# Windowed attention and a gated feed-forward layer: the down projection of tile pairs by Strassen's scheme, behind the ups, with a transposed output

## The chip, the core and the metric

One core of a Trainium2 chip. The metric is the device time in microseconds (us) of one execution, as the median of several runs. The core's engines are called as in the profile: PE (TensorE, matrix products; PEld is its weight load), DVE (VectorE), ACT (ScalarE, activations and copies), POOL (GpSimd), SP (SyncE, which starts the transfers here). The working memory is SBUF; PE writes to PSUM, eight banks of 128 x 512 float32.

## The reference

Eight batches and eight heads, 576 positions, head size 64, float32. Attention looks back over a window of 64 positions; its output, 4608 tokens of 512 numbers, is the input of a gated layer with 1536 hidden features.

```python
scores = scale * np.matmul(q, k.transpose(0, 1, 3, 2))
...
mask = (rel >= 0) & (rel < window)
scores = np.where(mask, scores, -1000000000.0)
scores = scores - np.max(scores, axis=-1, keepdims=True)
attn = np.exp(scores)
attn = attn / (np.sum(attn, axis=-1, keepdims=True) + 1e-09)
return np.matmul(attn, v).astype(np.float32)
...
x = np.ascontiguousarray(attn_out.transpose(0, 2, 1, 3)).reshape(B * S, H * D)
...
gate = 1.0 / (1.0 + np.exp(-(x @ w_gate)))
val = x @ w_val
return (gate * val @ w_out).astype(np.float32)
```

## The kernel before

**Tiles.** The tokens are cut into 12 tiles of 384 (`TT`), and these into 6 pairs. Activations stand feature by token: 128 features on the partitions, 384 tokens along the row. The 1536 hidden features are 12 blocks of 128, `j`; block `k` and block `k + 6` go together in a pair's products, so there are `NK` = 6 rounds. Every float32 operand of a large product is split in a high part (what PE's float32r format holds) and a low part, the rest. A product is three matmuls: high by high, high by low, low by high. A split is one copy (ACT) and one subtraction (DVE or POOL).

**Attention.** One unit is two heads of one tile, four units a tile. `stage_s` issues the scores on PE, and with them the outputs of the unit before; DVE takes the maxima (L232), ACT six exponentials (L241); `stage_n` divides by the sums (L259, POOL or DVE); `stage_b` transposes on PE (L290) and copies on ACT (L295); the outputs become the tile's input `xf`. The units of pair s + 1 are put between the products of pair s at planned places (`fill`, `attend`).

**The plain pair.** Pair 0 (tiles 0 and 1) is computed directly: `up` (L340) takes 12 matmuls of 128x384 for one block of gate or value, `gate_table` (L369) the sigmoid from ACT's table, `hidden_split` (L380) the two parts of the hidden block, `down` (L410) adds block j to the output of one group of 128 tokens: the hidden block is stationary, 512 columns of `w_out` move, three matmuls of 128x512. Tile 1's hidden blocks go to DRAM (`hd`) and come back when tile 0 has left its output banks. Beside this the weights, which arrive as float64, are converted (`conv_load` to `conv_c`, L97 to L143), and gate and value are written to DRAM as float32 (`w32d`) and in parts (`wd`).

**The five other pairs** take both up projections by Strassen's scheme in Winograd's form (`PRODUCTS`, L443): gate and value weights of round k are a 2 x 2 matrix of blocks (features by hidden features), the inputs of the two tiles another (features by tokens), and seven products of sums of blocks take the place of eight. A product is two halves of three matmuls of 128x384 (L579). The sums of the weights are made once, in the plain pair and in pair 1, on POOL (`sums_load`, `sums_make`, `sums_split`, `sums_store`, L477 to L528), in pieces of 128x128, and written to `wd`; later pairs read `wd` (`w_load`, seven buffers `W`). The input sums are made by `x_parts`, `x_part` and `x_rest`. In each round the seven products of the gate (m = 0) come first, then the seven of the value (m = 1), on three PSUM banks (`psum(s, b)`). `product` adds the results together on DVE (L585) and `result` makes of them a gate or a hidden block. In pairs 2 to 4 the gate is not the sigmoid: `gate_act` (L358) makes it of Relu, Tanh and Exp on ACT, a mask and a multiply on DVE, twice too large, which the output's copy makes good (L433).

**Their down projections** are plain ones. Tile a's (a = 2s) stand one after the other between the next round's products, on the other three banks; tile b's follow the last round (`last_tile`, L720), its hidden blocks split just ahead by `hidden_b` (L626). All 12 blocks of `w_out` stay in SBUF (`wo`).

**What sets the order.** The program is a list of events with planned times and a rank (`put`), sorted. PE keeps the order of the list (`keep_in_program_order`); the other engines' queues come from a scheduler which works on the list, with chains that hold ACT's table functions in order (`table_order`) and `issue_after`. SP starts all transfers in the order of its own queue, so a transfer that waits holds back those behind it.

## Time and profile before

| what | us |
|---|---|
| median of 3 runs (lowest to highest) | 1000.32 (999.86 to 1002.28) |
| span of the profiled execution | 997.6 |
| PE busy in it | 979.2 |
| start: attention of tiles 0 and 1, first weights | 0 to 48 |
| plain pair | 48 to 215 |
| pairs 1 to 5 begin at | 215, 377, 536.5, 696.5, 856.5 |
| down matmuls L419, all (804 + 402 + those of other forms) | 251.2 + 158.8 in the two large groups |
| transfers | 208.92 MB |

The profile shows one execution. The page's head gives the busy time of each engine; its groups name a line, an engine, an operation and the tiles (out<-in), with the number of instructions, the busy time and the mean time of one, and behind the bar the idle time of the engine just ahead of them with what ended it. The chain of work lists, from its start, what the end of the span depended on. A wait row reads "who L.. <- whom: us, count, longest". A table of windows has a row for each stretch and in it the busy time of every engine, the granted clock of PE (1.00 is full), the share in which the 16 DMA engines were busy, and what they moved. A matmul that is pipelined behind another costs PE the distance between their starts, which is less than the mean time that the groups give.

### The profile page before, as it was taken

Reading aid. Unit: us, or ns where it says so; the run is one execution under the profiler, and the core shown is the slowest. Engines: PE = TensorE matmul, PEld = TensorE weight load, DVE = VectorE, ACT = ScalarE, POOL = GpSimd, SP = SyncE. Lnnn points to the kernel's source line nnn. Section 1 sums busy time; section 2 is a strip of 40 time slices with the busy share of each in tenths; the row PEclk is TensorE's granted clock in tenths of the full one; section 3 lists DMA queues with packets and bytes.
Section 4 is the critical chain, followed back from the end, with each engine's and each line's share of the span. In section 5 each row is a group of like instructions: output and inputs, shape, how many; then the busy total and the mean of one; then the engine's idle time right before and its main releaser. Section 6 shows DMA issues by size and latency. Waiting matters only on the chain.

```text
span 997.6 us, 19847 instructions
## 1 busy us (share of the span) xinstructions
PE 979.2 (98%) x6984; PEld 884.1 (89%) x6984; DVE 633.0 (63%) x1737; ACT 530.5 (53%) x1433; POOL 253.5 (25%) x360
## 2 busy tenths in 40 slices
PE   7999999999999999999999999999999999999998
PEld 5888999889899889999988999988999997999996
DVE  7899888536665656666674666565666667344532
ACT  7888878544755646555545455464564464211122
POOL 4200124337674031112241122113212124010100
PEclk9999999999999999999999999999999999999999
DMA  9999888478786606766734776651776651466500
GB/s 336 320 346 364 321 286 278 144 258 292 262 259 219 221 33 225 228 218 218 219 108 130 229 233 209 213 196 38 242 237 214 203 187 56 161 224 195 190 32 32
DMA packets 84338, 208.92 MB, mean 209 GB/s; under 512 B 9360, under 2 KB 24976, under 8 KB 84240
## 3 DMA queue, kind: packets, MB, share of 16 engines
q1 hardware_dynamic: 84240, 207.66, 63.1%
q8 instruction: 56, 0.92, 0.4%
q14 instruction: 42, 0.34, 0.1%
HBM read 165.94 MB, written 41.68 MB: 208 GB/s over the span
## 4 chain that ended last, share of the span: by engine, by line
PE 84%; ACT 6%; DVE 4%; DMA 2%; issue 1%; DVEq 0%; ACTq 0%; SPq 0%
PE pr L579 40%; PE y L419 29%; PE ph L349 7%; PE s L208 3%; ACT p L241 3%; PE pp L290 3%; DMA w32d<-w 1%; PE s L319 1%; PE oo L319 1%; ACT g L362 1%; ACT e L361 1%; DVE p L232 1%; DMA wd<-w 1%; PE pr L319 1%; DVE u L585 0%
## 5 line engine op out<-in xcount | busy, mean ns | idle before, releaser
L419 PE MATMUL y<-w,hh 128*128 128x512 f32 x804 | 251.2, 393 | 0.0
L579 PE MATMUL pr<-x_T,wt 128*128 128x384 f32 x1152 | 226.4, 338 | 0.5
L579 PEld LDWEIGHTS pr<-x_T,wt 128*128 128x128 f32 x1152 | 202.2, 188 | 11.1 <-DVE u L585 4.3
L579 PE MATMUL pr<-x_B,wt 128*128 128x384 f32 x864 | 176.4, 340 | 0.2
L419 PEld LDWEIGHTS y<-w,hh 128*128 128x128 f32 x804 | 148.8, 189 | 21.8 <-ACT hh L384 1.4
L419 PE MATMUL y<-w,hl 128*128 128x512 f32 x402 | 158.8, 395 | 0.0
L579 PEld LDWEIGHTS pr<-x_B,wt 128*128 128x128 f32 x864 | 150.6, 188 | 8.2 <-issue 2.6
L585 DVE TENSOR_TENSOR u<-pr,p 128x384 f32<-128x384 f32 x120 | 66.5, 554 | 139.4 <-PE pr L579 138.8
L259 POOL TENSOR_TENSOR p<-p,rs 128x384 f32<-128x384 f32 x76 | 65.4, 875 | 288.2 <-DVE rs L250 197.4
L241 ACT ACTIVATE p<-p,mn 128x128 f32<-128x128 f32 x288 | 111.1, 393 | 27.1 <-DVE mn L232 26.3
L388 POOL TENSOR_TENSOR hl<-h,hh 128x384 fp32r<-128x384 f32 x48 | 50.0, 1042 | 283.8 <-DVE hh L386 283.8
L349 PE MATMUL ph<-x,w 128*128 128x384 f32 x576 | 105.9, 338 | 0.0
L349 PEld LDWEIGHTS ph<-x,w 128*128 128x128 f32 x576 | 99.7, 188 | 2.0 <-issue 1.0
L419 PEld LDWEIGHTS y<-w,hl 128*128 128x128 f32 x402 | 75.6, 188 | 18.3 <-DVE hl L388 2.1
L232 DVE CUSTOM_DVE_ANT_0 p<-s,m 128x128 f32<-128x128 f32 x288 | 66.3, 286 | 21.9 <-PE s L208 21.9
L585 DVE TENSOR_TENSOR c<-pr,u 128x384 f32<-128x384 f32 x120 | 66.7, 556 | 10.9 <-ACT g L372 4.8
L388 DVE TENSOR_TENSOR hl<-hb,hh 128x384 fp32r<-128x384 f32 x60 | 39.7, 673 | 41.2 <-ACT hh L384 40.7
L295 ACT COPY pT<-pp 128x384 f32<-128x384 f32 x96 | 41.5, 482 | 40.5 <-PE pp L290 40.3
L518 POOL TENSOR_TENSOR ws<-sw,ws 128x128 fp32r<-128x128 f32 x96 | 50.1, 556 | 36.2 <-ACT ws L514 30.7
L593 ACT COPY p<-pr 128x384 f32<-128x384 f32 x48 | 22.6, 471 | 68.5 <-PE pr L579 68.1
L384 ACT CAST hh<-hb 128x384 fp32r<-128x384 f32 x60 | 30.0, 512 | 50.9 <-PE y L419 50.7
L208 PE MATMUL s<-k,q 64*64 64x128 f32 x1152 | 47.5, 292 | 9.0 <-DMA k<-in_kT_dram 4.7
(95 smaller groups left out, 1402.8 us busy)
## 6 DMA issues: line engine op xcount, KB each, us to landing
wt<-wd SPq DMA_DIRECT2D x168, 512.0 KB, 4.1
v<-in_vN_dram SPq DMA_DIRECT2D x48, 384.0 KB, 4.4
wd<-ws SPq DMA_DIRECT2D x48, 256.0 KB, 4.0
k<-in_kT_dram SPq DMA_DIRECT2D x48, 224.0 KB, 4.5
q<-in_qT_dram SPq DMA_DIRECT2D x48, 192.0 KB, 4.2
wd<-w SPq DMA_DIRECT2D x36, 256.0 KB, 5.8
wa<-wd SPq DMA_DIRECT2D x36, 256.0 KB, 4.2
out_dram<-yo SPq DMA_DIRECT2D x33, 256.0 KB, 2.0
```

What stands on the lines that cost most here:

```text
L208: pe(nc.tensor.matmul(sc[h][half * BLK:(half + 1) * BLK, u, :], qt[h * BLK:(h + 1) * BLK, U * BLK:(U + 1) * BLK], kt[h * BLK:(h + 1) * BLK ...
L232: nc.vector.tensor_tensor_reduce(out=pt[:, u, :], in0=sc[:, u, :], in1=masks[key], op0=ALU.add, op1=ALU.min, scale=-SCALE, scalar=3.0e38, ...
L241: exp = nc.scalar.activation(pt[:, u, :], pt[:, u, :], AF.Exp, bias=mn[:, u:u + 1], scale=-1.0, **sums)
L259: eng.tensor_mul(out=pt, in0=pt, in1=rs.unsqueeze(2).broadcast_to([P, UP, P]))
L295: cp = nc.scalar.copy(pT, pp)
L349: pe(nc.tensor.matmul(ph, l, r, start=i == 0, stop=i == len(prs) - 1))
L384: nc.scalar.copy(h_hi, h32)
L388: return eng.tensor_sub(out=h_lo, in0=h32, in1=h_hi.bitcast(F32))
L419: pe(nc.tensor.matmul(yb[y], l, r, start=first and n == 0, stop=last and n == 2))
L518: nc.gpsimd.tensor_sub(out=w2[:, e, 1, cs], in0=sw[:, i + e, cs], in1=w2[:, e, 0, cs].bitcast(F32))
L579: pe(nc.tensor.matmul(ps, l, r, start=new and i == 0, stop=i == len(prs) - 1, skip_group_check=not new))
L585: nc.vector.tensor_add(out=o, in0=ps, in1=a)
```

## The change

**The down projection.** In pairs 1 to 5 it becomes Strassen's scheme too, and all of it follows the pair's ups. `w_out` of blocks k and k + 6 is a 2 x 2 matrix of blocks (hidden features by output features), the hidden blocks of the two tiles another (hidden features by tokens). `last_product` takes product n of round k: two halves q, each three matmuls of 128x384, with the weights stationary, so the output stands feature by token, `outT`, and the host turns it round. The six rounds of a product are added up in PSUM; at the last one `combine`, which the ups share, adds the products together, and `emit_out` writes. That makes 7 x 6 = 42 steps in a pair. Tiles 0 and 1 keep the plain `down` and an output of their own.

**Weights for it.** `wo_sums` makes the sums of `w_out` and their two parts for round k in the plain pair, 32 POOL instructions of 128x128 a round, and stores them; `wo_parts` stores the unsummed blocks; both to `wod`. `wo_load` reads 21 blocks of 512 KB in every pair, through seven buffers. `J_AT` changes the order in which the weight blocks are converted to 0, 6, 1, 7 and so on, so that k and k + 6 follow one another.

**Gate and value in lockstep.** A round's order becomes product by product, gate then value, each with three banks of its own (`psum(1 + m, b)`). The gate is the sigmoid in all pairs, and ACT's table functions are chained throughout.

**Splitting late.** The hidden blocks stay float32 in five buffers a round (`hidden`). `h_prep` makes two differences in place, and `h_part` makes the right-hand side of a step and splits it some eight steps ahead of it: the copy on ACT, the subtraction on POOL for two of the seven products and on DVE for the others. The inputs are treated in the same way (`differences`, `rhs_of`). DVE takes the subtraction of the value's weight sums (`sums_split`, m = 1). The last product of the last pair runs half by half, and its output is stored in two pieces.

```diff
+    def wo_sums(k):
+        cols = [slice(c, c + P) for c in range(0, H, P)]
+        b = [xp.tile([P, 3, H], F32, name=f"b{i}_{k}", tag=f"x{12 + i}") for i in range(2)]
...
+        for c in cols:
+            nc.gpsimd.tensor_add(out=b[0][:, 2, c], in0=b[0][:, 1, c], in1=b[1][:, 1, c])
...
+                nc.sync.dma_start(out=wo_at(k, name)[:, 0, :], in_=hi[:, e, :].bitcast(F32))
...
+        if m == 2 and j % 2:
+            put(tm + 5, 7.2, wo_sums, j // 2)
...
+    def wo_load(s, q):
+        w2 = wts.tile([P, 2, 2, H], F32R, name=f"wot_{s}_{q}", tag=f"wo_{q % WOB}")
+        nc.sync.dma_start(out=w2.bitcast(F32), in_=wod[q])
...
-            if plain_gate(t):
-                gate_table(t, j, c)
-            else:
-                gates[(t, j)] = gate_act(f"{t}_{j}", c)
...
+    def h_part(s, n, k):
+        src = rhs_of(nc.gpsimd, hidden(s, k), PRODUCTS[n][1])
+        h2 = xp.tile([P, 2, TT], F32R, name=f"h_{n}_{s}_{k}", tag=f"x{(n * NK + k) % (2 * NPR)}")
+        nc.scalar.copy(h2[:, 0, :], src)
+        eng = nc.gpsimd if n in (2, 6) else nc.vector
+        eng.tensor_sub(out=h2[:, 1, :], in0=src, in1=h2[:, 0, :].bitcast(F32))
+        hs[(s, n, k)] = h2
+
+    def last_product(s, n, k, qs=(0, 1)):
+        b = PRODUCTS[n][2]
+        for q in qs:
+            st = acc[q]
+            if n < 3 and k == 0 and not st.pop(("held", b), False):
+                st[b] = psum(1 + q, b, f"y{b}_{q}_{s}")
+            three(st[b][:, :TT], wot[(s, n, k)], q, hs[(s, n, k)], n < 3 and k == 0, k == NK - 1, n < 3)
+            if k == NK - 1:
+                combine(st, n, f"y{q}_{s}", lambda r, bb, in0, in1, q=q: emit_out(s, n, q, r, bb, in0, in1))
...
-            for m in range(2):
-                for n in range(NPR):
-                    put(now, 9, product, s, k, m, n)
-                    now += PRT
-                    if n in (2, 4, 6) and len(downs) > (RESERVE if m else 0) * (k == 1):
-                        j, x = downs.pop(0)
-                        put(now, 9, down, a, j, x, j == 0, False)
...
+            for n in range(NPR):
+                for m in range(2):
+                    put(now, 9, product, s, k, n, m)
...
+            for k in range(NK):
+                at_down.append(now)
+                put(now, 9, last_product, s, n, k)
+                now += PRT
+                attend(("d", NK * n + k))
+        for i, tm in enumerate(at_down):
+            put(t0 + i - 8 + (tm - t0 - PRT * i) if i > 7 else t0 + i - 8, 5.2, h_part, s, *divmod(i, NK))
+            if i % 2 == 0:
+                put(tm - 20, 8.2, wo_load, s, i // 2)
```

On POOL, in the plain pair, the normalizations of two units of attention follow one another (`p0_2_1`, `p1_2_1` for unit 1 of tile 2 and `p0_2_3` for its unit 3; `rs` are the sums of the exponentials, `sw_0_0` the gate's weight sums of round 0). Before, eight small instructions stand between them.

```order
L259 TENSOR_TENSOR p0_2_1_2023<-p0_2_1_2023,rs_2_1_2025 128x384
L259 TENSOR_TENSOR p1_2_1_2035<-p1_2_1_2035,rs_2_1_2025 128x384
L499 TENSOR_TENSOR sw_0_0_2612<-a1_0_0_2560 128x128 x2
L503 TENSOR_TENSOR sw_0_0_2612<-a0_0_0_2558,a1_0_0_2560 128x128 x2
L501 TENSOR_TENSOR sw_0_0_2612<-sw_0_0_2612,a0_0_0_2558 128x128 x2
L505 TENSOR_TENSOR sw_0_0_2612<-a0_0_0_2558,sw_0_0_2612 128x128 x2
L259 TENSOR_TENSOR p0_2_3_2275<-p0_2_3_2275,rs_2_3_2277 128x384
L259 TENSOR_TENSOR p1_2_3_2287<-p1_2_3_2287,rs_2_3_2277 128x384
```

Of the changed kernel these are the last rows of the same place; `b0_3`, `b1_3`, `bh0_3` and `bh1_3` are the sums of `w_out` for round 3 and their high parts.

```order
L484 CAST bh1_3_2157<-b1_3_2127 128x128
L486 TENSOR_TENSOR b1_3_2127<-b1_3_2127,bh1_3_2157 128x128
L486 TENSOR_TENSOR b0_3_2126<-b0_3_2126,bh0_3_2144 128x128
L515 TENSOR_TENSOR sw_0_0_2851<-a1_0_0_2800 128x128 x2
L486 TENSOR_TENSOR b1_3_2127<-b1_3_2127,bh1_3_2157 128x128
L519 TENSOR_TENSOR sw_0_0_2851<-a0_0_0_2798,a1_0_0_2800 128x128 x2
L486 TENSOR_TENSOR b1_3_2127<-b1_3_2127,bh1_3_2157 128x128
L517 TENSOR_TENSOR sw_0_0_2851<-sw_0_0_2851,a0_0_0_2798 128x128 x2
L268 TENSOR_TENSOR p0_2_3_2472<-p0_2_3_2472,rs_2_3_2474 128x384
L521 TENSOR_TENSOR sw_0_0_2851<-a0_0_0_2798,sw_0_0_2851 128x128
L268 TENSOR_TENSOR p1_2_3_2484<-p1_2_3_2484,rs_2_3_2474 128x384
```

A batch of `wo_sums` has come between them: 39 small instructions now stand there.

On PE, in the first round of pair 4 (`pr<bank>_<m>_<pair>_<round>` is the output of a product, m = 0 the gate; `wt` its weights, `x_..` its input by half). Before, these were products 4 to 7 of the gate, with the value's first behind them.

```order
L579 MATMUL pr1_0_4_0_8951<-x_T3_4_0_8785,wt_4_0_1_8740 128x384 x3
L579 MATMUL pr1_0_4_0_8951<-x_T3_4_1_8883,wt_4_0_1_8740 128x384 x3
L579 MATMUL pr0_0_4_0_8940<-x_B21_4_0_8796,wt_4_0_2_8767 128x384 x3
L579 MATMUL pr0_0_4_0_8940<-x_B21_4_1_8900,wt_4_0_2_8767 128x384 x3
L579 MATMUL pr1_0_4_0_8951<-x_T4_4_0_8807,wt_4_0_2_8767 128x384 x3
L579 MATMUL pr1_0_4_0_8951<-x_T4_4_1_8913,wt_4_0_2_8767 128x384 x3
L579 MATMUL pr2_0_4_0_8960<-x_B22_4_0_8820,wt_4_0_3_8791 128x384 x3
L579 MATMUL pr2_0_4_0_8960<-x_B22_4_1_8921,wt_4_0_3_8791 128x384 x3
L579 MATMUL pr0_1_4_0_9072<-x_B11_4_0_8752,wt_4_0_3_8791 128x384 x3
L579 MATMUL pr0_1_4_0_9072<-x_B11_4_1_8848,wt_4_0_3_8791 128x384 x3
```

The changed kernel from the same product on:

```order
L586 MATMUL pr1_0_4_0_9429<-x_T3_4_0_9319,wt_4_0_3_9203 128x384 x3
L586 MATMUL pr1_0_4_0_9429<-x_T3_4_1_9340,wt_4_0_3_9203 128x384 x3
L586 MATMUL pr1_1_4_0_9438<-x_T3_4_0_9319,wt_4_0_3_9203 128x384 x3
L586 MATMUL pr1_1_4_0_9438<-x_T3_4_1_9340,wt_4_0_3_9203 128x384 x3
L586 MATMUL pr0_0_4_0_9405<-x_B21_4_0_9355,wt_4_0_4_9234 128x384 x3
L586 MATMUL pr0_0_4_0_9405<-x_B21_4_1_9364,wt_4_0_4_9234 128x384 x3
L586 MATMUL pr0_1_4_0_9417<-x_B21_4_0_9355,wt_4_0_4_9234 128x384 x3
L586 MATMUL pr0_1_4_0_9417<-x_B21_4_1_9364,wt_4_0_4_9234 128x384 x3
L586 MATMUL pr1_0_4_0_9429<-x_T4_4_0_9376,wt_4_0_5_9262 128x384 x3
L586 MATMUL pr1_0_4_0_9429<-x_T4_4_1_9386,wt_4_0_5_9262 128x384 x3
L586 MATMUL pr1_1_4_0_9438<-x_T4_4_0_9376,wt_4_0_5_9262 128x384 x3
L586 MATMUL pr1_1_4_0_9438<-x_T4_4_1_9386,wt_4_0_5_9262 128x384 x3
```

Gate and value now alternate, on two sets of banks, and share one block of weights and one input.

400 lines of the change are left out of this document (226 added, 174 removed).

## The prediction

> **What bounds the kernel now.** I read the page's head first, then the busy time by stage, then what the matrix engine waited for, then the chain of work.
>
> ```profile
> span 997.6 us, 19847 instructions
> ...
> PE 979.2 (98%) x6984; PEld 884.1 (89%) x6984; DVE 633.0 (63%) x1737; ACT 530.5 (53%) x1433; POOL 253.5 (25%) x360
> ```
>
> PE is busy for 98% of the span, so time can come from two places only: less work on PE, or the 18 us in which it idles. The stages below are the start, the plain pair of tiles 0 and 1, and the five pairs by Strassen's scheme.
>
> ```profile
> core 0: us, PE busy (x) PEld busy (x) DVE busy (x) ACT busy (x) POOL busy (x), PEclk, DMA share, GB/s
> 0.00:48.00 48.00, 38.65 (x493) 32.48 (x494) 37.53 (x174) 40.11 (x120) 16.45 (x28) 0.96 0.92 330
> 48.00:215.00 167.00, 164.60 (x1191) 148.41 (x1190) 133.28 (x361) 123.02 (x282) 35.92 (x52) 0.99 0.83 287
> 215.00:377.00 162.00, 159.49 (x1130) 142.91 (x1129) 96.92 (x246) 91.81 (x226) 82.03 (x160) 1.00 0.66 215
> 377.00:536.50 159.50, 159.30 (x1154) 144.05 (x1153) 102.09 (x282) 83.29 (x252) 35.56 (x36) 1.00 0.60 190
> 536.50:696.50 160.00, 159.74 (x1155) 144.29 (x1154) 102.17 (x282) 82.10 (x251) 35.55 (x36) 1.00 0.59 190
> ...
> 856.50:997.60 141.10, 137.62 (x719) 127.99 (x718) 58.76 (x111) 28.03 (x56) 12.18 (x12) 1.00 0.45 146
> ```
>
> From 215 us on PE has almost no idle time, at a granted clock of 1.00, while DVE, ACT and POOL are busy for two thirds of it at most. In the plain pair (48 to 215) PE is as full, but there DVE and DMA are nearly full too, and the start is DMA and latency. Named waits of the products on other engines are small:
>
> ```profile
> PE pr L579 <- ACT g L372: 0.9, 1, 0.9
> ...
> PE pr L579 <- DVE u L585: 0.5, 1, 0.5
> ```
>
> **The gain: the down products.** For the cadence of one matmul I take long stretches of the chain of work in which PE does one thing.
>
> ```profile
> 824.14 32.18 PE y L419 x138
> 856.31 17.92 PE pr L579 x102
> ...
> 962.80 31.34 PE y L419 x138
> ```
>
> The down matmuls (512 columns) come every (32.18 + 31.34) / 276 = 0.2301 us, the product matmuls (384 columns) every 17.92 / 102 = 0.1757 us. A pair now needs 2 tiles x 12 rows of weights x 3 blocks x 3 = 216 of the first kind, 49.7 us. Afterwards it needs 7 products x 6 x 2 halves x 3 = 252 of the second kind, 44.3 us. That is 5.4 us a pair and **27.1 us** for the five. The plain pair keeps its 216 down matmuls.
>
> **The waits that go.** In the products, gate and value now alternate on six banks, so three products lie between two on one bank where one lay before. The waits above, 1.4 us, should go; the first of the Strassen pairs, which alone has the table gate and attention side by side, lasts 162.0 us against 159.5 for the next, so 2.5 us is the most that this can give, and nothing the least. I take **1.4 us**.
>
> **The gate on ACT and DVE.** The three activations, the mask and the multiply of Strassen pairs 2 to 4 become one sigmoid, at the price of 40 more table loads over the kernel.
>
> ```profile
> L241 ACT ACTIVATE p<-p,mn 128x128 f32<-128x128 f32 x288 | 111.1, 393 | 27.1 <-DVE mn L232 26.3
> ...
> L388 POOL TENSOR_TENSOR hl<-h,hh 128x384 fp32r<-128x384 f32 x48 | 50.0, 1042 | 283.8 <-DVE hh L386 283.8
> L241 ACT ACTIVATION_READ_ACCUMULATOR p<-p,mn 128x1 f32 x264 | 49.8, 189 | 0.0
> ...
> L388 DVE TENSOR_TENSOR hl<-hb,hh 128x384 fp32r<-128x384 f32 x60 | 39.7, 673 | 41.2 <-ACT hh L384 40.7
> ...
> L384 ACT CAST hh<-hb 128x384 fp32r<-128x384 f32 x60 | 30.0, 512 | 50.9 <-PE y L419 50.7
> ...
> L372 ACT ACT_TABLE_LOAD x17 | 21.8, 1283 | 1.0 <-DVE c L585 0.7
> ...
> L541 POOL TENSOR_TENSOR t<-xf,xf 128x384 f32<-128x384 f32 x8 | 9.3, 1168 | 44.5 <-DMA out_dram<-yo 33.2 <-ACT yo L433 11.3
> ```
>
> ACT is at 53%, so the 51 us of loads matter only where they stand in a row. At each attention unit ACT does two loads and six exponentials, then a gate and the two copies of a first product: 2 x 1.28 + 6 x 0.58 + 3 x 0.51 = 7.6 us. Queued behind is the copy on which the second product's sum, and so the fourth product, waits. PE meanwhile has the seventh, first, second and third product of both gate and value, 48 matmuls or 8.4 us. The margin is 0.8 us; I take no cost. If it is gone, PE waits about 1 us at each of the 24 units that lie in product phases.
>
> **The activations' split in the down part.** Each of the 42 steps of a pair gives PE 6 matmuls, 1.05 us, and needs one ACT copy (0.51), one subtraction on DVE (0.67) or POOL (1.04), and for 12 of them a difference on POOL (1.17). ACT and DVE have room. POOL does 12 x 1.04 + 12 x 1.17, and 10 x 1.17 for the last preparations of this pair and the next pair's inputs: 38 us within 44. The parts are made eight steps ahead on a ring of 14 buffers, and the differences of five of the six rows fall before the part begins, so I take nothing; the bounds are 0 and about 5 us a pair, what six late steps would cost. A gain is excluded, since nothing there was waited for.
>
> **The new work in the plain pair.** This is the cost that I do expect. Preparing sums of the down weights puts 192 instructions of 128x128 on POOL, six batches of 32, before 215 us, and 66 transfers on SP. What such an instruction costs depends on DVE:
>
> ```profile
> 195.89 3.76 POOL L518 TENSOR_TENSOR ws<-sw,ws 128x128 fp32r<-128x128 f32 x8
> ```
> ```profile
> 160.88 6.28 POOL L518 TENSOR_TENSOR ws<-sw,ws 128x128 fp32r<-128x128 f32 x8 [5.51 <-DMA hb<-hd]
> ```
> ```profile
> 164.03 0.62 DVE L386 CAST hh<-h 128x384 fp32r<-128x384 f32 x1
> 164.68 0.70 DVE L388 TENSOR_TENSOR hl<-h,hh 128x384 fp32r<-128x384 f32 x1
> ```
> ```profile
> 176.71 0.36 DVE L386 CAST hh<-h 128x384 fp32r<-128x384 f32 x1
> 177.10 0.56 DVE L388 TENSOR_TENSOR hl<-h,hh 128x384 fp32r<-128x384 f32 x1
> ```
>
> Alone, eight take 3.76 us (0.47 each); beside a working DVE 6.28 us (0.79 each). DVE's copy grew from 0.36 to 0.62 us beside them and its subtraction from 0.56 to 0.70; with one such instruction beside each, a POOL instruction costs DVE 0.14 to 0.26 us. I take 0.14, since the subtraction is like most of DVE's work there.
>
> ```profile
> 60.00:160.00 100.00, 97.82 (x720) 90.36 (x720) 90.16 (x236) 83.68 (x185) 17.64 (x20) 0.98 0.91 318
> ```
>
> Between 60 and 160 us DVE is busy for 90.2 of 100 us, and four batches fall there: 128 x 0.14 = 17.9 us more, of which 9.8 fit. So the plain pair would run up to 8 us longer on DVE's account. The other way in is POOL's own queue: PE's transposes wait for a normalization on POOL, which now stands behind a batch.
>
> ```profile
> 139.61 0.83 POOL L259 TENSOR_TENSOR p<-p,rs 128x384 f32<-128x384 f32 x1 [0.74 <-DVE rs L250]
> ...
> 154.35 1.03 POOL L259 TENSOR_TENSOR p<-p,rs 128x384 f32<-128x384 f32 x1 [0.54 <-DMA hd<-hl]
> ```
> ```profile
> 162.69 0.82 PE L290 MATMUL pp<-ident,p 128*128 128x128 f32 x6
> ```
>
> POOL is free at 140.4 and PE transposes at 162.7, 22.3 us later. The new order has 39 small instructions and two normalizations there: 39 x 0.47 + 1.9 = 20.2 us if alone, 39 x 0.79 + 1.9 = 32.7 us beside DVE. The transposes are on time or 10 us late. The two causes do not add, since a PE held back by DVE gives POOL time. The bounds are 0 and 18 us. I take **5 us**: DVE's 8, less what batches that wait for their own weights leave it free. The transfers go to a DMA that moves 318 GB/s at a share of 0.91 there: 21 blocks of 512 KB are 11 MB, 31 us of DMA time, and the 167 us at 0.83 have 28 us to spare. I count the remaining 3 us as hidden, since they fall on stores that nobody awaits soon; they are inside the 18.
>
> **The transfers of the pairs.** The down weights no longer stay on the chip.
>
> ```profile
> wt<-wd SPq DMA_DIRECT2D x168, 512.0 KB, 4.1
> v<-in_vN_dram SPq DMA_DIRECT2D x48, 384.0 KB, 4.4
> ...
> k<-in_kT_dram SPq DMA_DIRECT2D x48, 224.0 KB, 4.5
> q<-in_qT_dram SPq DMA_DIRECT2D x48, 192.0 KB, 4.2
> ```
>
> A pair now reads 42 blocks of 512 KB; afterwards 63. The extra 11 MB on 190 GB/s over 160 us (30 MB at a share of 0.60) make 41 MB in 154 us, a share of about 0.85. In the down part alone a block serves 2.1 us of PE and seven are held, 14.8 us ahead against 4.1 us of landing. Hidden, then; if the cover is gone, see the second rival.
>
> **The end.** The last output is now added in two halves by DVE where ACT and DVE copied halves: equal.
>
> **The sum.** The profiled execution's span is 997.6 us and the median of the three runs 1000.3, so 2.7 us lie around it. 997.6 - 27.1 - 1.4 + 5 = 974.1, and with 2.7 us around it **976.8 us**.
>
> **The rivals.**
>
> [...] Chance 0.07.
>
> *The down part starves.* Fourteen of its 21 blocks (seven come earlier), the next pair's first seven, three attention units of 0.8 MB and 1.6 MB of output come to 15 MB in some 46 us, 326 GB/s, where 190 GB/s had a share of 0.60, so 317 at most. Backlog of a few us a pair, or POOL's six late steps, gives 4 us x 5 = 20: 997 at the worst and 990 as the middle. For it: the shares. Against it: 14.8 us of lead. Chance 0.15.
>
> *The table loads bind.* One us at 24 units: 1000.8 if the margin is wrong everywhere, but it is positive, so a third of that: 985. Chance 0.06.
>
> *The change does not do what it says* is excluded: the order shows 1260 matmuls of 384 columns for 1080 of 512.
>
> **The numbers.** The forecast has 0.72. Its own range is 968 (no cost in the plain pair, 2.5 us of waits gone) to 990 (18 us). The second rival reaches 997; to leave out no more than 2 in 10 the range goes from **967 to 992**. A change under 0.3% (3 us) can't be told from none here. Faster by more: all of the forecast, 0.11 of the starving, 0.05 of the loads, 0.88. Within: 0.04 of the starving and 0.01 of the loads, 0.05. Slower: 0.07.
>
> **What the changed profile would show.** Pairs of some 154 us (377 to 531 and so on), the last of 135.7, with PE full. In the plain pair, PE's waits for POOL's normalizations and DVE at over 95% between 60 and 160 us. Right if the products follow the plain pair at about 220 us instead of 215. Wrong if that moves by over 18 us (the ports), if down parts last much over 44.3 us plus their attention (starving), or if products wait for ACT copies (loads).

## The result, and the profile after

The changed kernel takes 1014.0 us (median of 4 runs, 1010.89 to 1014.62), the kernel before 1001.3 us beside it: a ratio of 1.012 (95% interval 1.0097 to 1.0144). It is slower, by 1.2%, where 976.8 us were forecast. The profiled execution took 1010.89 us with a span of 1009.1; it is the quickest of the four, so its rows show some 3 us less of the loss than the median does.

The page's head: PE has 22 us less work than before (979.2) and idles 52 us instead of 18, and POOL's work has grown from 253.5 us.

```profile
span 1009.1 us, 20697 instructions
...
PE 956.9 (95%) x7164; PEld 904.2 (90%) x7164; DVE 686.3 (68%) x1681; ACT 588.5 (58%) x1469; POOL 482.3 (48%) x626
```

The same stages as in the prediction, in the changed kernel:

```profile
core 0: us, PE busy (x) PEld busy (x) DVE busy (x) ACT busy (x) POOL busy (x), PEclk, DMA share, GB/s
0.00:48.00 48.00, 37.63 (x495) 31.79 (x496) 37.78 (x174) 40.16 (x120) 16.41 (x28) 1.00 0.89 330
48.00:215.00 167.00, 153.11 (x1102) 137.92 (x1101) 150.06 (x336) 117.01 (x261) 133.33 (x212) 0.98 0.96 329
215.00:377.00 162.00, 155.39 (x1166) 143.22 (x1166) 113.51 (x280) 100.62 (x257) 98.17 (x166) 1.00 0.86 294
...
536.00:696.00 160.00, 154.91 (x1199) 148.69 (x1199) 99.81 (x250) 94.42 (x246) 64.58 (x62) 1.00 0.81 261
...
856.00:1009.00 153.00, 146.94 (x837) 146.04 (x836) 85.52 (x143) 49.16 (x100) 45.30 (x42) 0.99 0.66 215
```

In the plain pair PE idles 13.9 us instead of 2.4, POOL is busy for 133 us instead of 36. In 160 us of the later pairs PE now idles 5.1 us, where it idled 0.3 before. The chain of work gives the place at which the pairs begin. Its piece starts at the second matmul; the first starts at 231.6 us, and at 214.7 in the kernel before (the 214.9 of the expectations below is the second one there):

```profile
227.44 4.31 PE y L411 x18
231.75 4.19 PE pr L586 x24
```

From the first product of each pair to that of the next, worked out from the starts of PE's matmuls:

| | first product | pair 1 | pair 2 | pair 3 | pair 4 | pair 5 |
|---|---|---|---|---|---|---|
| before | 214.7 | 162.1 | 159.5 | 159.9 | 160.0 | 141.5 |
| changed | 231.6 | 161.1 | 159.9 | 158.4 | 158.9 | 139.2 |
| forecast | about 220 | | 154 | 154 | 154 | 135.7 |

So the plain pair lost 16.9 us instead of 5, and the five pairs gave 5.4 us instead of 28.5. Both have to be explained.

**The plain pair.** DVE's five large groups of it, from 48 to 215 us, in the changed kernel and in the one before:

```profile
L128 DVE SCALAR_TENSOR_TENSOR w<-w,zz 128x512 int32<-128x512 int32 x31 | 25.9, 839 | 0.4
L158 DVE TENSOR_TENSOR w<-w,w 128x512 fp32r<-128x512 f32 x32 | 25.4, 797 | 2.8 <-ACT w L157 2.7
L130 DVE CUSTOM_DVE_ANT_0 w<-raw,w 128x1024 uint16<-128x1024 uint16 x31 | 25.3, 818 | 0.3
L126 DVE TENSOR_SCALAR zz<-w 128x512 int32<-128x512 int32 x30 | 18.1, 608 | 4.7 <-ACT w L117 4.5
L380 DVE TENSOR_TENSOR hl<-h,hh 128x384 fp32r<-128x384 f32 x23 | 17.1, 745 | 0.3
L386 DVE TENSOR_TENSOR h<-ph,g 128x384 f32<-128x384 f32 x22 | 12.0, 545 | 0.4 <-ACT w L157 0.2 <-PE ph L358 0.2
```
```profile
L147 DVE TENSOR_TENSOR w<-w,w 128x512 fp32r<-128x512 f32 x32 | 22.7, 711 | 1.2 <-ACT w L146 1.2
L123 DVE SCALAR_TENSOR_TENSOR w<-w,zz 128x512 int32<-128x512 int32 x31 | 21.5, 708 | 0.1
L125 DVE CUSTOM_DVE_ANT_0 w<-raw,w 128x1024 uint16<-128x1024 uint16 x31 | 21.4, 695 | 0.0
L121 DVE TENSOR_SCALAR zz<-w 128x512 int32<-128x512 int32 x30 | 13.9, 473 | 1.5 <-ACT w L112 1.3
L388 DVE TENSOR_TENSOR hl<-h,hh 128x384 fp32r<-128x384 f32 x23 | 13.2, 573 | 0.4
L394 DVE TENSOR_TENSOR h<-ph,g 128x384 f32<-128x384 f32 x22 | 12.1, 550 | 4.1 <-PE ph L349 2.6 <-ACT g L372 1.6
```

The same 147 instructions take 111.8 us instead of 92.7. POOL issued 160 instructions more there (212 for 52), so each lengthened DVE by 0.12 us on average. L386 (L394 before), whose one operand lies in PSUM, keeps its 0.55 us.

From 48 us to the first product PE has the same matmuls in the same order in both kernels. Before and after:

```profile
48.00:214.68 166.68, 164.28 (x1189) 148.10 (x1188) 133.13 (x361) 122.95 (x281) 35.92 (x52) 0.99 0.83 286
48.00:231.59 183.59, 168.80 (x1187) 149.72 (x1186) 157.62 (x359) 121.02 (x276) 145.23 (x236) 0.98 0.96 336
```

PE idles 14.8 us instead of 2.4, and its own work takes 4.5 us longer, at a granted clock of 0.98 for 0.99. It hardly waits for DVE itself (1.1 us): it waits for ACT, and ACT for DVE's conversion. The rows from 48 to 232 us; the last is of the kernel before.

```profile
PE s L219 <- ACT xf L316: 5.5, 4, 3.2
PE ph L358 <- ACT g L367: 2.9, 2, 1.5
PE oo L328 <- ACT pT L304: 2.3, 2, 2.1
ACT w L157 <- DVE w L130: 27.7, 20, 3.8
ACT w L146 <- DVE w L125: 7.8, 10, 1.2
```

Waits for POOL's normalizations, which the prediction feared, are 1.8 us.

**The later pairs.** Products hardly wait; down matmuls do. The groups of the page:

```profile
L586 PE MATMUL y<-h,wot 128*128 128x384 f32 x1260 | 231.0, 341 | 15.3 <-DVE h L673 5.9
...
L586 PE MATMUL pr<-x_T,wt 128*128 128x384 f32 x1224 | 226.1, 336 | 1.4 <-DVE c L596 1.2
```

The waits stand at the seam between a pair's last up product and its down products. The timeline of PE and of POOL there, in pair 3 (its last product ends at 656.5 us):

```profile
657.50 5.48 PE L586 MATMUL y<-h,wot 128*128 128x384 f32 x30 [0.99 <-ACT xf L282]
663.76 0.55 PE L299 MATMUL pp<-ident,p 128*128 128x128 f32 x3 [0.78 <-POOL p L268]
...
674.44 0.44 PE L586 MATMUL y<-h,wot 128*128 128x384 f32 x1 [1.42 <-ACT h L671]
676.06 2.20 PE L586 MATMUL y<-h,wot 128*128 128x384 f32 x11 [1.18 <-DVE h L673]
```
```profile
664.46 2.29 POOL L673 TENSOR_TENSOR h<-h,h 128x384 fp32r<-128x384 f32 x2
666.71 1.34 POOL L549 TENSOR_TENSOR h<-h 128x384 f32<-128x384 f32 x1
668.01 3.29 POOL L673 TENSOR_TENSOR h<-h,h 128x384 fp32r<-128x384 f32 x3
671.26 1.31 POOL L550 TENSOR_TENSOR h<-h,h 128x384 f32<-128x384 f32 x1
672.54 1.30 POOL L557 TENSOR_TENSOR h<-h,h 128x384 f32<-128x384 f32 x1
```

L549 and L550 are the two differences of the last round's hidden blocks, L557 makes from the first of them the right-hand side of product 1's sixth step (products are counted from 0 here, as in the code). Five subtractions of product 2 (L673), which PE needs later, stand before and between them on POOL; ACT's copy of L557's result comes at 673.9 us, and PE waits for it at 674.4.

### The profile page after: what moved, and what is told of

Read it like the earlier page. It is cut to its first block, busy times and chain, and to the rows that moved or that the text cites. A ratio compares the mean times of both kernels' runs of the same rounds, so it can differ in the third digit from the quotient of the medians.

```text
span 1009.1 us, 20697 instructions
## 1 busy us (share of the span) xinstructions
PE 956.9 (95%) x7164; PEld 904.2 (90%) x7164; DVE 686.3 (68%) x1681; ACT 588.5 (58%) x1469; POOL 482.3 (48%) x626
## 4 chain that ended last, share of the span: by engine, by line
PE 63%; DVE 18%; ACT 8%; DMA 4%; POOL 3%; issue 3%; SPq 0%; DVEq 0%; POOLq 0%; ACTq 0%
PE pr L586 35%; PE y L586 17%; DVE h L673 7%; PE ph L358 3%; ACT p L251 2%; PE s L219 2%; PE pp L299 2%; PE y L411 2%; DVE h L629 2%; DVE w L130 1%; PE s L328 1%; POOL h L673 1%; DVE w L128 1%; DVE w L158 1%; ACT h L671 1%
## 5 line engine op out<-in xcount | busy, mean ns | idle before, releaser
L586 PE MATMUL y<-h,wot 128*128 128x384 f32 x1260 | 231.0, 341 | 15.3 <-DVE h L673 5.9
L586 PEld LDWEIGHTS y<-h,wot 128*128 128x128 f32 x1260 | 222.1, 191 | 19.8 <-DVE h L673 7.2
L671 ACT CAST h<-h 128x384 fp32r<-128x384 f32 x210 | 100.9, 513 | 79.3 <-PE y L586 39.6
L673 DVE TENSOR_TENSOR h<-h,h 128x384 fp32r<-128x384 f32 x150 | 115.6, 803 | 41.8 <-ACT h L671 41.7
L367 ACT ACTIVATE g<-c 128x384 f32<-128x384 f32 x90 | 47.3, 525 | 141.2 <-DVE c L625 141.0
L629 DVE TENSOR_TENSOR h<-c,g 128x384 f32<-128x384 f32 x90 | 64.5, 716 | 39.2 <-ACT g L367 33.3
L673 POOL TENSOR_TENSOR h<-h,h 128x384 fp32r<-128x384 f32 x60 | 64.7, 1088 | 53.8 <-ACT h L671 52.9
L596 DVE TENSOR_TENSOR c<-pr,p 128x384 f32<-128x384 f32 x60 | 33.1, 551 | 55.1 <-PE pr L586 55.1
L549 POOL TENSOR_TENSOR h<-h 128x384 f32<-128x384 f32 x21 | 23.7, 1128 | 65.7 <-DVE h L629 65.7
L299 PE MATMUL pp<-ident,p 128*128 128x128 f32 x288 | 43.9, 282 | 9.6 <-POOL p L268 6.8
L219 PEld LDWEIGHTS s<-k,q 64*64 64x64 f32 x1152 | 34.4, 140 | 18.6 <-ACT xf L316 6.4
```

The source lines that it names most:

```text
L219: pe(nc.tensor.matmul(sc[h][half * BLK:(half + 1) * BLK, u, :], qt[h * BLK:(h + 1) * BLK, U * BLK:(U + 1) * BLK], kt[h * BLK:(h + 1) * BLK ...
L299: pe(nc.tensor.transpose(pp[:, u, :], pt[:, u, :], ident))
L367: act = nc.scalar.activation(g, c, AF.Sigmoid)
L586: pe(nc.tensor.matmul(ps, l, r, start=first and i == 0, stop=last and i == 2, skip_group_check=not check))
L629: nc.vector.tensor_mul(out=hidden(s, k)[2 * r + b], in0=c, in1=gates.pop((t, j)))
L671: nc.scalar.copy(h2[:, 0, :], src)
```

## The experiments

Two questions: what cost the plain pair 16.9 us, and what cost the pairs their gain. "First product" is the start of pair 1's first product matmul, as in the table above. Three kernels were run once only (so marked) and are read by their traces; the others were timed in several rounds beside the kernel before, and have a ratio to it with its 95% interval.

How far can a first product be trusted? Six traces have the same plain pair, in the same order on PE, ACT, DVE and POOL: the changed kernel and five runs below that alter only what comes later, or when some stores are made. Their first products are at 231.6, 232.5, 233.3, 233.6, 233.6 and 234.3 us. So a difference of under 3 us between two single traces says little. And where an edit takes sums or stores out of the plain pair, PE's order stays but the scheduler sorts the queues of ACT and DVE anew; no run changes that order alone with sums or stores in place.

### The plain pair: sums, stores or order

**Without POOL's sums.** The stores stay.

```diff
     def wo_sums(k):
...
-        for c in cols:
-            nc.gpsimd.tensor_add(out=b[0][:, 2, c], in0=b[0][:, 1, c], in1=b[1][:, 1, c])
...
+        for i, names in enumerate((("S3", "S1"), ("S4", "S2"))):
+            src = wo_all[2 * k + i].bitcast(F32)
+            for e, name in enumerate(names):
+                for part in range(2):
+                    nc.sync.dma_start(out=wo_at(k, name)[:, part, :], in_=src[:, part, e * H:(e + 1) * H])
```

> The changed kernel without the 192 POOL instructions of wo_sums; the same 66 transfers to wod are made, of the unsummed blocks of w_out (the sums are left out, so the output is not the reference's). Theory A, POOL's small instructions cost the plain pair its time (they lengthen DVE's and stand ahead of the normalizations): the first product of the Strassen pairs starts at 217 us or before instead of 231.6, the span falls from 1009 to about 995, DVE's mean for L130 (now 0.818 us) goes back to about 0.70. Rival B, the transfers and SP's queue cost it: the first product stays at 228 or later, the span at 1006 or more.

Measured: 1003.54 us, ratio 1.0023 (1.0008 to 1.0038); first product at 224.4 us. DVE's L130 is back at 0.72 us. Neither theory is met: POOL's instructions account for 7.1 us of the first product (10.5 by the medians), and 9.8 us stay. ACT still waits for L130 for 20.9 us in 18 waits, though L130 has nearly its old time. The stages from 48 us on show the DMA engines full (shares in the kernel before: 1.01, 0.84 and 0.63):

```profile
48.00:103.00 55.00, 51.32 (x362) 47.17 (x361) 46.24 (x125) 42.53 (x94) 5.55 (x5) 0.94 1.01 350
103.00:167.00 64.00, 64.00 (x472) 59.56 (x471) 53.72 (x137) 49.56 (x109) 12.33 (x16) 1.00 1.01 346
167.00:215.00 48.00, 44.50 (x305) 37.17 (x305) 34.62 (x90) 28.70 (x70) 8.95 (x17) 0.96 1.03 374
```

**Without the stores.** POOL's instructions stay.

```diff
-                nc.sync.dma_start(out=wo_at(k, name)[:, 0, :], in_=hi[:, e, :].bitcast(F32))
-                nc.sync.dma_start(out=wo_at(k, name)[:, 1, :], in_=b[i][:, a, :])
...
-        put(now - 24 + 2 * k, 8.6, wo_parts, k)
...
-        nc.sync.dma_start(out=w2.bitcast(F32), in_=wod[q])
+        nc.sync.dma_start(out=w2.bitcast(F32), in_=wd[q % NK][(0, 4, 5)[q // NK % 3]])
```

> The changed kernel with wo_sums' POOL instructions but none of the 66 transfers to wod; the loads of the pairs read blocks of wd of the same size instead (so the output is not the reference's). Theory A: the first product stays at 228 us or later, the span at 1006 or more. Rival B: the first product at 217 or before, the span about 995. If both have a part, the sum of the gains of this run and of the one without POOL's instructions is near 16.7 us, what the plain pair lost.

Measured: 1023.24 us, ratio 1.0216 (1.0199 to 1.0233); first product at 243.7 us, 12 us later than with the stores (9 by the medians). Theory A's words hold, and rival B falls in this form, but the two gains don't add up to 16.9 at all: 7.1 and minus 12.1. So this run doesn't price the stores by themselves. POOL waited for a store for only 1.1 us in the changed kernel, but without stores its queue comes in another order: the third normalization, for one, stands behind 35 instructions of the sums in a row where it stood behind 24. PE's transposes wait for normalizations among them. One such wait, and their sum between 48 and 232 us (total, times, longest):

```profile
96.14 0.90 PE L299 MATMUL pp<-ident,p 128*128 128x128 f32 x3 [3.90 <-POOL p L268]
```
```profile
PE pp L299 <- POOL p L268: 12.0, 6, 3.9
```

**Without both, and in the old order.** The first leaves out the sums and the stores; the second also puts back the order of the conversions.

```diff
-    J_AT = [j // 2 + (j % 2) * NK for j in range(NF)]
+    J_AT = list(range(NF))
```

> The changed kernel without wo_sums' POOL instructions and without the 66 transfers to wod; the loads of the pairs read blocks of wd instead (so the output is not the reference's). Without the POOL instructions alone the first product of the pairs came at 224.4 us, 9.6 us behind the 214.9 of the kernel before. Theory T, these 9.6 us are the transfers, which fill the DMA engines (share 1.01 to 1.03 there): the first product comes at 217 or before. Rival O, they come from the new order of the conversions and the other edits of the plain pair: it stays at 222 or later.

> The run without sums and transfers, and with the weight blocks converted in the old order 0, 1, 2 and so on (the sums and stores of w_out are left out, so the output is not the reference's). Theory T: within 1.5 us of the run without sums and transfers. Rival O: the first product comes earlier than in that run by most of what is left over 214.9 us.

Measured, one run each: first product at 215.8 and 216.5 us (999.01 and 994.51 us in all). Theory T's number is met: without sums, the stores cost 8.6 us (224.4 to 215.8), and the new order of the conversions costs the plain pair nothing (0.7 us the other way). Sums and stores together explain 15.8 of the 16.9 us. The DMA share in the three stages of the first of the two is 0.95, 0.90 and 0.80, against 1.01, 1.01 and 1.03 with the stores. What carries the 8.6 us is not shown by this. ACT's waits for transfers are small in both (3.2 us each for the stores to `w32d`), while its waits for L130 fall from 20.9 us in 18 to 7.8 in 10, as many as in the kernel before, and its queue is in another order. Full DMA is one reading, the order of ACT's and DVE's queues the other. That the second run is 4.5 us quicker in all lies in its pairs (776.0 us for 781.2) and stays unexplained.

**Normalizations on DVE**, once with everything else of the changed kernel but product 2's subtractions (which are explained below), once in the run without stores.

```diff
-        eng = nc.vector if t == 3 and p % 2 or t // 2 == 2 else nc.gpsimd
+        eng = nc.vector if t // 2 in (1, 2) else nc.gpsimd
```

> The run with product 2's subtractions on DVE (994.1 us), and with the 12 normalizations of tiles 2 and 3 that POOL makes in the plain pair on DVE. Theory Q, the normalizations in POOL's queue behind the sums hold PE back (delays of 1.8, 1.7 and 3.1 us at three transposes): the first product comes 4 us or more earlier than at 233.6, the median at about 990. Rival D, DVE's lengthened work is the bound: 12 more instructions of 0.6 us make the plain pair longer by some us, the median at 996 or more.

> The run without the transfers to wod (first product at 243.7 us, output not the reference's for the same reason), with the 12 normalizations of tiles 2 and 3 on DVE. Theory Q: without the stores POOL's sums follow one another without a break, and the normalizations queue behind them; PE waited 12.0 us for these in six waits. On DVE those waits go, and the first product comes at 233 or before. Rival D: DVE's lengthened work is what binds there too; the first product stays at 240 or later.

Measured: 996.74 us, ratio 0.9953 (0.9936 to 0.9969), first product at 234.6 us where it was 233.6; and, one run, first product at 240.6 us where it was 243.7. In both the waits for POOL's normalizations are gone and others have come. Theory Q falls as the whole cause, and rival D's figures are met in both (996 or more; 240 or later), though 1.0 and 3.1 us between single traces are about as much as equal plain pairs differ. In the second run the longest of the new waits shows another carrier. PE waits 7.0 us for ACT's copy of the transposes, and ACT waits for the last batch of sums:

```profile
206.09 0.51 ACT L574 CAST x_B<-xf 128x384 fp32r<-128x384 f32 x1 [8.12 <-POOL b L486]
206.51 0.85 ACT L304 COPY pT<-pp 128x384 f32<-128x384 f32 x2
```

L574 makes pair 1's inputs, some of them in the buffers `x10` to `x13`, in which `wo_sums` works. Its copy waits for the last batch, and the transposes' copies stand behind it on ACT.

**Lighter sums, fewer stores.** The first takes product 2's subtractions on DVE, keeps the converted block (no adding up of its parts) in five rounds and copies the high parts on ACT, 104 POOL instructions instead of 192; the split of the sums becomes an event of its own, 6 us later in the list. The next two move 12 stores of 256 KB into pair 1, with the full and with the light sums.

```diff
-                    nc.gpsimd.tensor_copy(out=hi[:, e, c], in_=b[i][:, a, c])
+                nc.scalar.copy(hi[:, e, :], b[i][:, a, :])
...
+        if m == 2 and j < 10:
+            b = xp.tile([P, 3, H], F32, name=f"b{j}", tag=f"x{12 - 4 * (j // 2 % 2) + j % 2}")
+            w32 = b[:, 0:2, :].rearrange("p a h -> p (a h)")
...
-        put(now - 24 + 2 * k, 8.6, wo_parts, k)
+        put(now + 20 + 10 * k if k < 4 else now - 24 + 2 * k, 8.6, wo_parts, k)
```

> The changed kernel with product 2's subtractions on DVE, as in the run that did this alone (994.1 us), and with lighter sums: in five of six rounds the converted block is kept instead of being added up from its parts, and the high parts are copied by ACT, so that 104 POOL instructions of 128x128 are left of 192 in the plain pair. Theory P, POOL's instructions cost the plain pair in proportion: of the 7.1 us that leaving all of them out gave, about 3.3 come back, the first product at about 230 us instead of 233.6, the median about 990.5. Rival W, they cost by when they stand in the way of single waits: the first product moves by less than 1 or by more than 6 us.

> The run with product 2's subtractions on DVE (994.1 us), with the stores of the unsummed blocks of w_out for rounds 0 to 3 (12 transfers of 256 KB) moved from the end of the plain pair into pair 1. Theory T, the plain pair is short of DMA (share 0.96; the 66 transfers alone, without sums, cost it 8.6 us): 3 of 11 MB leave it, and the first product comes 2 to 3 us earlier than at 233.6, the median at about 991.5. Rival D, with the sums present DVE is the bound and the transfers are hidden beside it: the first product moves by less than 1 us.

> The run with light sums (993.4 us, first product at 231.1) and the 12 stores of unsummed blocks moved into pair 1. Theory T: with light sums the plain pair is short of DMA (share 1.0), so 3 MB less bring the first product to 229 or before, and the median to about 991. Rival D: as with the full sums, no change (231 and 993.4).

Measured: 993.36 us, ratio 0.9916 (0.9893 to 0.9938), first product at 231.1 us; 993.58 us, 0.9930 (0.9915 to 0.9945), at 233.6; 992.93 us, 0.9923 (0.9906 to 0.9940), at 230.9. With light sums four traces have the first product at 229.8 to 231.1 us (the two light ones here, and the two of "What is left at the seam"), six with the full sums at 231.6 to 234.3: 2 to 3 us for nearly half of POOL's instructions, about what theory P names. Little of it reaches the end: pair 1 takes 159.8 us instead of 158.6, and the median is 0.7 us less, within the intervals, where P had 990.5. Moving 3 of the 11 MB gives nothing with either kind of sums, against theory T and as rival D says. With the full sums all four queues of the plain pair keep their order in that run, so it is the cleaner test of the DMA.

### The later pairs: attention at the seam, or POOL's splits

**Attention unit 6 behind the ups.**

```diff
-                visit(("u", NPR * v - 2), 3, *unit(s + 1, v), unit(s + 1, v - 1), spare_up)
-            visit(("d", 10), 3, *unit(s + 1, 7), unit(s + 1, 6), lambda s=s: spare_down(s))
+                at, spare = (("u", NPR * v - 2), spare_up) if v < 6 else (("u", 41), spare_6)
+                visit(at, 3, *unit(s + 1, v), unit(s + 1, v - 1), spare)
+            visit(("d", 11), 3, *unit(s + 1, 7), unit(s + 1, 6), lambda s=s: spare_down(s))
...
```

> The changed kernel with attention unit 6's scores behind the last up product of a pair instead of ahead of it (and its outputs beside a bank that is needed later), its transposes at step 6 instead of 4, unit 7 one step later. Theory S1, the unit's exponentials and table loads stand ahead of the last gate on ACT and its normalization in POOL's queue, and this makes the first down steps late: PE's idle time of about 5.0 us a pair (pairs 2 to 4) falls to 2 or less, the span by 10 to 15 us to about 996. Rival S2, the preparation of the hidden parts by itself (POOL's and DVE's differences and subtractions) is too slow at the seam: idle time stays at 4 us or more a pair, the span within 3 us of 1009.

Measured: 1015.63 us, ratio 1.0149 (1.0132 to 1.0165). PE still idles 5.2 us in pair 2 (160.3 us long, 155.1 busy). Theory S1 falls. Of rival S2 the idle time is met, the span (1013.1 for 1009 within 3) not quite.

**Product 2's subtractions on DVE.**

```diff
-        eng = nc.gpsimd if n in (2, 6) else nc.vector
+        eng = nc.gpsimd if n == 6 else nc.vector
```

> The changed kernel with the subtraction of product 2's six hidden parts a pair on DVE instead of POOL. Theory S1: no gain, since what is late is the gate (span within 2 us of 1009, or some us longer, as DVE has more to do). Rival S2, with POOL's queue as its cause: the two waits of 1.4 and 1.2 us near the sixth step vanish, and the span falls by about 2.5 us a pair, 10 us in all.

Measured: 994.08 us, ratio 0.9929 (0.9914 to 0.9944): faster than the kernel before. Pairs of 158.6, 155.7, 155.7, 154.6 and 134.8 us, 18.0 us less in sum than in the changed kernel, though the first product is at 233.6 us. Rival S2 holds, and gives more than it promised. POOL and the stages of pairs 2 and 3:

```profile
660.49 1.26 POOL L549 TENSOR_TENSOR h<-h 128x384 f32<-128x384 f32 x1 [0.49 <-DVE h L629]
661.83 1.22 POOL L550 TENSOR_TENSOR h<-h,h 128x384 f32<-128x384 f32 x1
663.02 1.32 POOL L557 TENSOR_TENSOR h<-h,h 128x384 f32<-128x384 f32 x1
```
```profile
392.20:547.90 155.70, 152.99 (x1190) 147.10 (x1190) 101.70 (x257) 93.37 (x244) 56.28 (x54) 1.00 0.82 266
547.90:703.60 155.70, 152.94 (x1190) 147.08 (x1189) 101.69 (x257) 93.38 (x244) 56.32 (x54) 1.00 0.82 267
```

From L549's start to L557's end it is 3.9 us instead of 7.1, and PE's waits of 1.4 and 1.2 us at the sixth step are gone (idle 2.7 us a pair for 5.1). DVE's own work in such a pair rises by 2 us only (101.7 for 99.8), though it makes six more subtractions: others are lengthened less.

**All subtractions on DVE, and three products' on POOL.**

```diff
-        eng = nc.gpsimd if n in (2, 6) else nc.vector
+        eng = nc.vector                                        # the first
+        eng = nc.gpsimd if n in (2, 4, 6) else nc.vector       # the second
```

> The changed kernel with all 42 subtractions of a pair on DVE (it has two products' on POOL, 1014.0 us; one product's gave 994.1). Theory C, a subtraction on POOL lengthens DVE's beside it by about as much as DVE needs for it and comes late itself: no loss against one product's, pairs of 155 to 156 us, the median at 992 to 995. Rival F, DVE is full in the down part: six more of 0.56 us make a pair 2 us or more longer, the median at 1002 or more.

> The changed kernel with three products' subtractions on POOL (2, 4 and 6) instead of two. Theory C: POOL gets 6 more instructions of 1.1 us in each down part, and lengthens DVE's: pairs longer again by 2 to 4 us, the median at 1024 to 1034. Rival S, only the place of product 2's at the seam hurts: the median within 3 us of 1014.

Measured: 994.53 us, ratio 0.9938 (0.9922 to 0.9955), pairs of 155.7 us; and 1018.23 us, ratio 1.0172 (1.0156 to 1.0187), pairs of 159.7 to 161.8 us from the second to the fourth. Product 6's place on POOL is worth nothing, product 4's costs some 4 us in all, product 2's 18 to 20 us. So it is the place more than the number: product 2 is prepared at the seam. Theory C holds for the first run, and for the second only in part (1018 for 1024 to 1034; rival S's 1014 within 3 isn't met either). What it says of DVE is to be checked in the group of DVE's subtractions from 392 to 1000 us, with one, two and three products' on POOL:

```profile
L673 DVE TENSOR_TENSOR h<-h,h 128x384 fp32r<-128x384 f32 x144 | 104.9, 774 | 14.0 <-ACT h L671 13.9
```
```profile
L673 DVE TENSOR_TENSOR h<-h,h 128x384 fp32r<-128x384 f32 x120 | 94.9, 821 | 34.7 <-ACT h L671 34.6
```
```profile
L673 DVE TENSOR_TENSOR h<-h,h 128x384 fp32r<-128x384 f32 x96 | 82.5, 889 | 47.1 <-ACT h L671 46.9
```

The rising mean is no price by itself. With none on POOL it is already 0.74 us, and it rises also because the groups hold other products. By product, in pairs 2 and 3: product 0's subtractions take 1.09 us on DVE in all four kernels, product 5's 0.55 to 0.59; product 3's take 0.68 us with none or one product on POOL, 1.10 with product 2 there and 1.23 with product 4 as well. So DVE is lengthened where POOL works at the same time, at product 3.

**What is left at the seam.** With light sums and fewer stores in both: first, unit 5's outputs go beside another bank (one that is still being added up at that time, so the values are not the reference's; the work is the same); second, unit 6 is transposed at down step 6 instead of 4.

```diff
-                visit(("u", NPR * v - 2), 3, *unit(s + 1, v), unit(s + 1, v - 1), spare_up)
+                visit(("u", NPR * v - 2), 3, *unit(s + 1, v), unit(s + 1, v - 1), spare_6 if v == 6 else spare_up)
```
```diff
-[(("u", 41), ("d", 4)), (("d", 12), ("d", 18))]
+[(("u", 41), ("d", 6)), (("d", 12), ("d", 18))]
```

> The run with light sums (993.4 us) with the same stores moved, and with the outputs of unit 5 beside a bank that the down products use later, so that the first down product does not wait for their copies. If the plain pair is short of DMA with light sums (share 1.0 there), the first product comes 3 us or more earlier than at 231.1; the wait of 1.0 us ahead of each pair's first down product goes, 0.8 to 1.0 us in each of four pairs; the median at about 987. If neither is on the path: 993 as before.

> The same with the transposes of attention unit 6 at down step 6 instead of 4. If PE's two waits for the normalizations (1.0 and 0.2 us a pair) are only early transposes, they go without another wait in their place: pairs 2 to 4 last 154.5 instead of 155.7 us, the median 4 to 5 us less than in the run before it. Rival: the next wait takes their place, as when the whole unit was moved; within 1 us a pair.

Measured: 993.79 us, ratio 0.9930 (0.9915 to 0.9945), pairs 2 and 3 of 156.6 us; and 992.89 us, ratio 0.9921 (0.9898 to 0.9944), pairs of 155.4 us. Neither gives the gain: idle time is 2.5 us in both, another wait of the attention's chain having come in place of the one removed (in the first, 2.0 us for ACT's `xf` ahead of a late up product, where 1.0 us stood ahead of the first down product; in its pairs 2 to 4 PE's own work also takes 1.1 us longer, at a granted clock of 0.99). The last is the lowest median here, 8 us under the kernel before, but its interval overlaps with those of the six other kernels at 993 to 995.

## Why the prediction was wrong, point by point

The span was forecast at 974.1 us and came to 1009.1. Of the 35.0 us, 11.9 lie in the plain pair and 23.1 in the five others. (A slip in the range changes nothing here: its lower end of 968 leaves out the 2.7 us around the span that the other sums have, and should be 971.)

- **The gain of the down products** was right in mechanism and about right in size. With product 2's subtractions on DVE, PE's own work falls by 6 to 7 us in pairs 2 and 3 (forecast 5.4). They take 155.7 us for the forecast 154, with 2.7 us of idle time left, and the last takes 134.8 for 135.7.
- **The waits that go** (1.4 us): not to be seen; the products of the changed kernel wait 2.1 us, all for DVE's sums, which is no less than the 1.4 us before. Within its bounds of 0 and 2.5, at their low end.
- **The table loads** were rightly taken at nothing: no product waits for ACT in the changed kernel.
- **The activations' split in the down part** is the first step that failed. "The differences of five of the six rows fall before the part begins, so I take nothing": the sixth row is what matters. Its differences are made on POOL after the last product, and the order of POOL's queue puts five subtractions of a later product before and among them. The sum of POOL's work (38 us within 44) was no measure of this, since a chain at one place waits whatever the sum. I took nothing, with 5 us a pair as the bound; moving these subtractions gave 18.0 us for the five pairs, 3.6 each.
- **The plain pair** is the second: 16.9 us where 5 were taken, inside the bounds of 0 and 18 in this trace, up to 19.6 in the five with the same plain pair. DVE's growth was sized well (0.12 us for each POOL instruction, against 0.14). What failed is the path. The step "of which 9.8 fit" sets DVE's growth against DVE's idle time: DVE is busy for 150 of 167 us, so there was room. But ACT stands between: its waits for the conversion grow from 7.8 to 27.7 us, and PE waits 10.7 us for ACT's copies and gates. The path that was named, POOL's normalizations, is worth 1.8 us, and DVE is busy for 93% from 60 to 160 us, not over 95. Nor did I count that PE's own work would take 4.5 us longer. And "I count the remaining 3 us as hidden" failed: without sums, adding the 66 stores cost 8.6 us, whether by full DMA or by the queues' new order.
- **DVE's loss beside POOL**: in the plain pair it was 0.12 us for each POOL instruction, near the 0.14 of the forecast and far from the 0.47 us that such an instruction takes alone. The kernel is slower, to which the forecast gave 0.07, but not by such a price. Not all of DVE's instructions were lengthened: L386, with its operand in PSUM, kept 0.55 us. The 0.12 us are an average over all of POOL's instructions, also those that met none of the lengthened ones on DVE, so they are no price of a single meeting; a subtraction grew there from 0.55 to as much as 1.41 us (last section).
- **The starving rival** was the nearest to what came: not for DMA, as its name says (no down matmul of the pairs waited for its weights), but for "POOL's six late steps", its second half. It stood alone at 990 to 997 us, and the plain pair's bound at 18 us stood in the forecast's own range. Both ends came together, and both come at least in part from giving more work to POOL beside a busy DVE: I should have treated them as one case, 997.6 - 28.5 + 18 + 20 + 2.7 = 1010 us, instead of reading each end as a single miss.

What stays open: how the plain pair's loss divides once POOL's instructions are nearly halved (231 us, with DMA full, at shares of 0.99 to 1.01, and PE's clock at 0.94 and 0.93 in two of three stages). The trace of that run names the waits: PE waits 9.6 us for ACT's copy `xf` (5.6 and 3.8 in two of them) and 2.1 for `pT`, and ACT waits 16.5 us for DVE's conversion and 2.7 in one piece for POOL's weight sums, just ahead of the second of these copies. No run moved ACT's copies alone, so that its queue is the cause, rather than full DMA, is argued and not shown. How much belongs to the buffers shared between the last batch of sums and pair 1's inputs is open too; other buffers were not tried. That removing the stores alone makes the pair 12 us longer is shown; that this comes from POOL's new order is argued from the waits in that trace, and the run with the normalizations off POOL (3 of the 12 us, little more than the spread) doesn't confirm it.

## What to carry to other kernels

Where an engine takes over "free" work, don't compare sums of busy time over a stage: write down, at the place where the next engine is first in need, what stands in that engine's queue ahead of the needed instruction. Here one word, the engine of one product's six subtractions, decided between 1014 and 994 us. Follow the chain through the engine in between, too: PE lost its time in the plain pair mostly waiting for ACT, which waited for DVE. And when two uncertain costs have the same source, their upper ends belong in one case with a chance of its own.

## What the runs showed of the hardware

**Behind some short stops the granted clock was 0.50.** In the last pair of the changed kernel PE stops twice for 1.2 us. The timeline of PE, and a window of 5 us with the granted clock:

```profile
970.01 0.44 PE L586 MATMUL y<-h,wot 128*128 128x384 f32 x1 [1.18 <-ACT h L671]
971.63 8.70 PE L586 MATMUL y<-h,wot 128*128 128x384 f32 x41 [1.18 <-DVE h L673]
```
```profile
970.00:975.00 5.00, 3.81 (x13) 3.56 (x14) 5.00 (x8) 1.71 (x4) 1.94 (x2) 0.66 0.21 78
```

From 972.1 to 974.4 us matmuls come every 0.32 us, at a granted clock of 0.50, then again every 0.173. With the slow ones at both ends, nine take 2.97 us (971.6 to 974.6) instead of 1.56: about 1.4 us lost beside the 2.4 us of idle time. So a pair gained more than its idle time when these stops went (4.4 us in the last pair, 2.6 of it idle time). The slow stretch came behind two stops of 1.2 us with one matmul between them; at the same place in pair 3 (1.4 and 1.2 us) the rate stayed full, at a granted clock of 1.00. Pairs 2 and 4 have such a stretch of 3.4 us (granted clock 0.50 from 517.1 and from 834.5 us), right behind two such stops (1.4 and 1.2 us). In the run with unit 5's outputs beside another bank it follows a single stop of 2.0 us in each of pairs 2 to 4; the mean granted clock of that run is 0.986, where it was 0.991 with light sums alone. What decides whether such a stretch comes is not shown.

**Beside POOL, DVE's subtractions in SBUF were lengthened, and its instructions with an operand in PSUM were not.** In the changed kernel 403 instructions of DVE on 128x384 add, subtract or multiply with one operand in PSUM; they take 0.53 to 0.56 us each, 0.55 in the mean both for the 157 that ran beside POOL and for the 246 that ran alone. A subtraction of 128x384 with both operands in SBUF (L673) takes 0.55 us, 0.56 at most, when POOL is idle beside it, and up to 1.41 us when POOL works; in the changed kernel 57 of DVE's 150 ran alone and 93 beside POOL, with a mean of 0.96 us. POOL's own subtraction goes from 1.02 us alone to 1.13 in the mean and 1.40 at most beside DVE.
